# Gated MLP after softcap attention on one core: first queries' transfers on two queues, an early table load, a last fill unit in the scores' banks, another bank for v unit 0

## The chip, the cores and the metric

One NeuronCore of a Trainium2 chip runs the whole kernel. The metric is the device time of one execution in microseconds; a lower number is better. The time before is the median of three runs; a further execution was profiled.

## The reference

Two batches of 12 heads, 448 positions, 64 features per head. Softcap attention, a gMLP block with a spatial gate, and a convolutional gated MLP follow each other:

```python
scores = cap * np.tanh((scale * q @ k.T) / cap)
attn = np.exp(scores - scores.max(-1, keepdims=True))
attn = attn / (attn.sum(-1, keepdims=True) + 1e-09)
x = heads_side_by_side(attn @ v)                       # 448 x 768
h = gelu_tanh(x @ w_in)                                # 448 x 1024
u, v = h[..., :512], h[..., 512:]
v_n = (v - mean(v)) / sqrt(var(v) + 1e-06) * g_ln
x = x + (u * (w_sg @ v_n + b_sg)) @ w_out
h = np.maximum(x @ w2_in, 0.0)
out = h * sigmoid(depthwise_conv3(h, conv_w)) @ w2_out
```

Everything is float32, the weights of the two MLPs float64.

## The kernel before

Every product is made of three TensorE (PE) products: an operand is split into a `hi` part of reduced precision and the `lo` rest, and hi·hi, hi·lo and lo·hi are added up in PSUM. ScalarE (ACT) and VectorE (DVE) make the splits. The float64 weights come in as words in pieces; each piece is decoded by ACT and DVE in three or four operations (`decode`, `decode_half`; tile `f`).

*Attention* works on 12 pairs of heads, two rounds R per pair. `scores` multiplies K by Q into four PSUM banks (tag "sc"), ACT takes the tanh and the exponential (tile `raw`), and `values` multiplies `raw` by V and by ones into three banks (tag "pv"), the sums beside the values. The eighth bank (pool `psm`, tag "mo") is left for other work. The sums are inverted and spread over the partitions by a way through DRAM, but for the last pair, where `norm_pe` inverts them on DVE and `spread` does the spreading by four products on PE; these go to the instruction lists in recording order (`ordered`).

*The head.* `load(0)` starts the transfers of the first pair: Q's two halves (partitions 0 to 63 and 64 to 127) through SP's queue, the first 256 columns of K's halves through ACT's. `WARM` matmuls on a tile of zeros (`wz`) occupy PE until the first operands are ready. `prep_k(0)` splits K on DVE, `prep_q(0)` splits Q with ACT (hi) and DVE (lo), `constants` makes the cap's reciprocal, which scales the first tanh. ACT's first activation brings a table load with it.

*The fill units.* The table FILL puts the first four units of the next product (u = X·w_in, batch 0, i = 0 to 3) between the last rounds of the attention. Unit 1 takes a bank of the scores (`free`, name "fi"), the others the `psm` bank. `u_done` takes the gelu, in four steps, the last on DVE (L231, tile `u`).

*Behind the attention*, `rest` runs a list of units (`seq`): u of batch 0 (the four already done), v units 0 to 2, u of batch 1, v units 3 to 6, eight spatial-gate units (`sg_unit`), twelve output units (`o_unit`). v unit 3, "v3" below, is the one on the gathered last rows of both batches (`XS`, in the tile GH). Each unit takes a bank by `bank(n)`: the one `psm` bank for n < 4 and for n % 4 == 3, the seven of `ps1` else. A v unit is evacuated by ACT (square, L224), DVE (L227), ACT (tanh), DVE (L231), and then normalised; a gate unit by DVE (`gt`), ACT (GH, the hi half) and DVE (`gl`, the lo half), from which the output units multiply. In this part a scheduler that simulates the program's timing sets the order of each engine's instructions, from the recording and the tiles' dependences; `pin` forces an instruction behind another.

In the names of the rows the number of a buffer is left out, and L392 is the one line through which all ordered products go.

Of the kernel before, what the change touches and what calls it, by code (L numbers as in the profile page):

```python
# [37 lines left out]

TAKEN = 4

WARM = 13

K0 = 2 * P

# [9 lines left out]
def stages(  # L54
# [46 lines left out]
    def f(ap):  # L101
        return ap.bitcast(F32)
# [30 lines left out]
    ub = [c0]  # L133

    heads = []

    def decode_half(hi, lo, src, pool, bufs, wait, hi_eng, top_eng):

        n = src.shape[1]
        r = pool.tile([P, 512, 2], U32, tag="f64", name="f64", bufs=bufs)[:, :n]  # L140
        words = r.rearrange("p c w -> p (c w)").bitcast(U16)
        sync(words[:, : 4 * n - 1], src.rearrange("r c w -> r (c w)").bitcast(U16)[:, 1:])
        low = r[:, :, 0]
        top = words.rearrange("p (c w) -> p c w", w=4)[:, :, 2].bitcast(BF16)
        heads.append(heads.pop(0))
        hd = heads[-1][:, :n]

        def s1():
            half = hd.bitcast(F16).rearrange("p (c w) -> p c w", w=2)[:, :, 1]
            with pin(lasta), pin(lastv):  # L150
                if top_eng == "a":
                    A.activation(half, top, AF.Copy)
                else:
                    V.tensor_copy(half, top)

        def s2():
            V.scalar_tensor_tensor(
                out=low, in0=low, scalar=13, in1=hd, op0=ALU.logical_shift_right, op1=ALU.bitwise_or
            )
            if hi_eng == "a":  # L160
                A.activation(hi, f(low), AF.Copy)
            else:
                V.tensor_copy(hi, f(low))

        def s3():
            V.tensor_tensor(out=lo, in0=f(low), in1=f(hi), op=ALU.subtract)

        for k, fn in zip(wait, (s1, s2, s3)):
            later(k, fn)
# [111 lines left out]
    def attention(att, psa):  # L281
# [10 lines left out]
        def load(n):  # L292
            b, p = divmod(n, NPAIR)
            qr = att.tile([P, S], F32, tag="qr", name="qr", bufs=3)
            kr = kraw[n % 2]
            for h in range(2):
                r = slice(h * D, (h + 1) * D)
                sync(qr[r], qT[b, p, r, h])

            k0 = 0 if n else K0  # L300
            if k0:
                nc.scalar.dma_start(kr[:D, :k0], kT[b, p, :D, 0, :k0])
                nc.scalar.dma_start(kr[D:, :k0], kT[b, p, D:, 1, D : D + k0])
            sync(kr[:D, k0:], kT[b, p, :D, 0, k0:])
            sync(kr[D:, k0:ST], kT[b, p, D:, 1, D + k0 :])
            sync(kr[D:, ST:], kT[b, p, D:, 1, :D])
            qraw[n] = qr, kr
# [9 lines left out]
        def prep_q(n):  # L317
            qr, _ = qraw[n]
            q = Qt[n] = att.tile([P, 2, S], F32R, tag="Q", name="Q", bufs=2)
            if n == 0:  # L320

                lasta[0] = A.activation(q[:, 0], qr, AF.Copy)  # L322
                with pin(lastv):
                    lastv[0] = V.tensor_tensor(out=q[:, 1], in0=qr, in1=f(q[:, 0]), op=ALU.subtract)
                return
            V.tensor_scalar(out=q[:, 0], in0=qr, scalar1=qscale[:, 0:1], scalar2=None, op0=ALU.mult)
            lastv[0] = V.scalar_tensor_tensor(
                out=q[:, 1], in0=qr, scalar=qscale[:, 0:1], in1=f(q[:, 0]),
                op0=ALU.mult, op1=ALU.subtract,
            )  # L330
# [28 lines left out]
        if WARM:  # L359

            wz = att.tile([P, S], F32R, tag="rb", name="wz", bufs=2)
            V.memset(f(wz), 0.0)
            wps = psa.tile([P, 4, 512], F32, tag="sc", name="wps", bufs=1)[:, 0, :S]
            for i in range(WARM):
                T.matmul(wps, lhsT=wz[:, :P], rhs=wz, start=True, stop=True)
        prep_k(0, slice(0, K0))
        prep_q(0)
        constants(att)
        creg = A.alloc_register("creg")
        with pin(lasta):  # L370
# [27 lines left out]
        def scores(N, half, then=None):  # L398
# [28 lines left out]
            for g in range(2 * half, 2 * half + 2):  # L427
# [3 lines left out]
                c = slice(g * P, (g + 1) * P)  # L431
                if g < 3:

                    for i, (j, l) in enumerate(((0, 0), (1, 0), (0, 1)) if N == 0 else ((0, 0), (0, 1), (1, 0))):
                        for h in range(2):
                            r = slice(h * D, (h + 1) * D)
                            out, x = to[:, g * 2 + h, :S] if g < 2 else ps[:, h, :2], q[r, l]
# [152 lines left out]
        def norm_pe(N, both):  # L590

            b, p = divmod(N, NPAIR)
            both_e = att.tile([P, 2 * (S + HS)], F32, tag="E", name="E", bufs=3)[:, S + HS :]
            A.activation(both_e, both, AF.Copy)
            e, r = both_e[:, :S], both_e[:, S:]
            V.tensor_scalar(out=r, in0=r, scalar1=guard, scalar2=None, op0=ALU.add)
            V.reciprocal(out=r, in_=r)

            def spread():
                rp = sums[:, :S]  # L600
# [14 lines left out]
        for R in range(2 * NN + LAGS[1] + 1):  # L615
# [40 lines left out]
            if R in FILL:  # L656

                i, k0, k1 = FILL[R]
                if k0 == 0:
                    if i == 1:  # L660
                        free = psa.tile([P, 4, 512], F32, tag="sc", name="fi", bufs=1)
                    fill[i] = free[:, i, :S] if i == 1 else psm.tile([P, 512], F32, tag="mo", name="mo")[:, :S]
                for k in range(k0, k1):
                    mmw(fill[i], 0, i, k, ordered)
                if k1 == NK:
# [81 lines left out]
    def rest():  # L747
# [3 lines left out]
        with ExitStack() as s1:  # L751
# [16 lines left out]
                G.tensor_copy(XS[:, :, :, b * D : (b + 1) * D], f(X[:, :, :, b, ST:S]))  # L768

            def bank(n):  # L770
                return (psm if n < 4 or n % 4 == 3 else ps1).tile([P, 512], F32, tag="mo", name="mo")

            ub.append(c1)

# [312 lines left out]
```

## Time and profile before

| what | value |
|---|---|
| median of 3 runs | 326.25 us (325.84 to 326.45) |
| the profiled execution's own time | 326.67 us |
| its span | 324.9 us |
| PE busy | 315.0 us, 97% |
| DVE busy | 243.5 us, 75% |
| ACT busy | 219.8 us, 68% |
| share of PE in the chain that ended last | 94% |

The span is the time from the first to the last instruction that the profiler recorded; 1.8 us of the execution's own time lie outside it. A busy share is an average over stages: a stage's own limit is read from the rows of that stage, and the chain that ended last shows which wait was the last to end. Start times are counted from the span's start.

### The profile page before, as it was taken

The page shows a single profiled execution, that of the slowest core. Times are in us where ns is not written, and L with a number is a line of the kernel's source. Part 1 is how long each engine was busy: PE and PEld are TensorE (multiplying, and loading weights), DVE is VectorE, ACT ScalarE, POOL GpSimd, SP SyncE. Part 2 cuts the span into 40 slices and gives each one's busy share as a digit, 9 for nine tenths or more (in the row PEclk, how much of TensorE's full clock was granted, in tenths as well). Part 3 has the DMA queues.
Part 4 walks back from the last instruction along what each step waited for, and adds up shares of the span by engine and source line. Part 5 has one row for each costly group of instructions (what it writes and reads, how often), then busy time and mean ns, then how long its engine had stood idle before and what let it go on. Part 6 is the DMA issues. An engine that isn't in the chain of part 4 may idle for free.

```text
span 324.9 us, 6285 instructions
## 1 busy us (share of the span) xinstructions
PE 315.0 (97%) x2377; PEld 260.8 (80%) x2377; DVE 243.5 (75%) x485; ACT 219.8 (68%) x353; POOL 36.5 (11%) x73
## 2 busy tenths in 40 slices
PE   6999999999999999999999999999999999999992
PEld 5566666666677789988999999999999999999991
DVE  2749698598576899999997889996788999990000
ACT  2999999898973457767765655555667988883010
POOL 4001042241341120211111000000000000000000
PEclk9999999999999999999999999999999999999998
DMA  3567976955542253122223670002490123013111
GB/s 111 133 197 207 248 217 145 247 150 179 168 126 69 59 167 108 50 69 95 67 72 126 203 295 0 2 1 65 130 372 19 32 67 97 1 55 141 63 59 34
DMA packets 22222, 37.73 MB, mean 116 GB/s; under 512 B 7352, under 2 KB 14536, under 8 KB 22184
## 3 DMA queue, kind: packets, MB, share of 16 engines
q1 hardware_dynamic: 20392, 34.51, 34.8%
q0 software_dynamic: 1632, 2.61, 2.9%
q8 instruction: 20, 0.33, 0.4%
q14 instruction: 18, 0.15, 0.2%
q10 hardware_dynamic: 160, 0.13, 0.1%
HBM read 34.40 MB, written 2.79 MB: 114 GB/s over the span
## 4 chain that ended last, share of the span: by engine, by line
PE 94%; ACT 2%; DMA 1%; DVE 1%; SPq 0%; issue 0%; ACTq 0%
PE mo L114 18%; PE mo L112 18%; PE mo L113 18%; PE pv L392 15%; PE sc L392 10%; PE mo L392 4%; PE mo L791 3%; PE mo L793 3%; PE mo L792 3%; DMA qr<-in_qT_dram 1%; PE fi L392 1%; ACT raw L409 1%; PE mo L837 1%; PE mo L838 0%; ACT L322 0%; DVE u L231 0%
## 5 line engine op out<-in xcount | busy, mean ns | idle before, releaser
L113 PE MATMUL mo<-X,WI 128*128 128x448 f32 x120 | 43.7, 366 | 0.0
L114 PE MATMUL mo<-X,WI 128*128 128x448 f32 x120 | 43.7, 365 | 0.0
L112 PE MATMUL mo<-X,WI 128*128 128x448 f32 x120 | 43.1, 366 | 0.0
L418 ACT ACTIVATE raw<-raw 128x1344 f32<-128x1344 f32 (+2 forms) x25 | 36.4, 1461 | 0.7
L114 PE MATMUL mo<-HG,W 128*128 128x448 f32 x96 | 34.7, 365 | 0.0
L113 PE MATMUL mo<-HG,W 128*128 128x448 f32 x96 | 34.6, 366 | 0.0
L409 ACT ACTIVATE raw<-sc 128x1792 f32<-128x1792 f32 (+1 forms) x22 | 32.5, 1475 | 2.0 <-PE sc L392 1.8
L112 PE MATMUL mo<-HG,W 128*128 128x448 f32 x96 | 33.3, 366 | 0.0
L392 PE MATMUL pv<-raw,V 128*32 128x224 f32 x576 | 32.9, 358 | 0.0
L182 ACT ACTIVATE f<-f 128x256 f32<-128x256 f32 (+2 forms) x44 | 22.9, 520 | 12.9 <-DMA f<-in_w_in_dram 7.1
L192 DVE SCALAR_TENSOR_TENSOR f<-f 128x256 uint32<-128x256 uint32 (+2 forms) x44 | 22.4, 518 | 9.2 <-ACT f L185 8.9
L392 PE MATMUL sc<-Q,K 64*128 64x448 f32 x210 | 27.7, 385 | 0.4 <-ACT raw L409 0.4
L392 PEld LDWEIGHTS pv<-raw,V 128*32 128x32 f32 x576 | 18.8, 109 | 11.6 <-issue 5.5
L392 PEld LDWEIGHTS sc<-Q,K 64*128 64x128 f32 x210 | 17.9, 185 | 9.7 <-ACT raw L409 5.5
L112 PEld LDWEIGHTS mo<-X,WI 128*128 128x128 f32 x120 | 22.5, 188 | 1.9
L113 PEld LDWEIGHTS mo<-X,WI 128*128 128x128 f32 x120 | 22.5, 188 | 1.9
L114 PEld LDWEIGHTS mo<-X,WI 128*128 128x128 f32 x120 | 22.5, 188 | 1.8
L185 ACT ACTIVATE f<-f 128x256 uint32<-128x256 uint32 (+2 forms) x44 | 22.6, 514 | 0.0
L195 DVE SCALAR_TENSOR_TENSOR f<-f 128x256 uint32<-128x256 uint32 (+2 forms) x44 | 22.4, 514 | 0.1
L971 ACT ACTIVATE o<-mo 128x448 f32<-128x448 f32 x12 | 6.3, 543 | 22.3 <-PE mo L114 18.9
L112 PEld LDWEIGHTS mo<-HG,W 128*128 128x128 f32 x96 | 18.0, 188 | 1.6
L114 PEld LDWEIGHTS mo<-HG,W 128*128 128x128 f32 x96 | 18.0, 188 | 1.4
(155 smaller groups left out, 694.9 us busy)
## 6 DMA issues: line engine op xcount, KB each, us to landing
f<-in_w_in_dram SPq DMA_DIRECT2D x12, 512.0 KB, 4.0
f<-in_w_out_dram SPq DMA_DIRECT2D x24, 256.0 KB, 5.0
f<-in_w_in_dram SPq DMA_DIRECT2D x12, 511.8 KB, 5.8
f<-in_w_out_dram SPq DMA_DIRECT2D x8, 384.0 KB, 3.1
qr<-in_qT_dram SPq DMA_DIRECT2D x24, 112.0 KB, 4.3
out_dram<-o SPq DMA_DIRECT2D x12, 224.0 KB, 2.0
rb<-d POOLq DMA_DIRECT2D x22, 112.0 KB, 3.5
V<-in_vL_dram SPq DMA_DIRECT2D x12, 192.0 KB, 3.4
```

The source lines that it names most:

```text
L112: matmul(ps, lhsT=whi, rhs=xhi, start=start, stop=False)
L113: matmul(ps, lhsT=whi, rhs=xlo, start=False, stop=False)
L114: matmul(ps, lhsT=wlo, rhs=xhi, start=False, stop=stop)
L182: A.activation(f(h), f(h), AF.Copy, scale=2.0**-112)
L185: A.activation(l, l, AF.Copy, scale=0.93 * 2.0**-29)
L192: V.scalar_tensor_tensor(out=l, in0=h, scalar=3, in1=l, op0=ALU.logical_shift_left, op1=ALU.bitwise_or)
L195: V.scalar_tensor_tensor(out=l, in0=h, scalar=0x80000000, in1=l, op0=ALU.bitwise_and, op1=ALU.bitwise_or)
L392: lastm[0] = T.matmul(*args, **kw)
L409: lasta[0] = A.activation(x, ps, AF.Tanh, **sc)
L418: lasta[0] = A.activation(x, x, AF.Exp, scale=creg)
L791: T.matmul(ps, lhsT=xs(0, k), rhs=WI[1][:, 0, k], start=k == 0, stop=False)
L792: T.matmul(ps, lhsT=xs(0, k), rhs=WI[1][:, 1, k], start=False, stop=False)
```

## The change

Eight edits:

1. `load(0)` starts Q's half 0 through ACT's queue and half 1 through SP's, each as the first of its queue; the K halves come second, half 0 through ACT's, half 1 through SP's.
2. A one-column exponential of the zeros is recorded right behind their memset, so that the table load stands there.
3. `prep_q(0)` is recorded ahead of `prep_k(0)`, which is pinned behind Q's lo half on DVE; the first pair's products take hi·hi, K hi·Q lo, K lo·Q hi, as the other pairs do.
4. `WARM` goes from 13 to 12.
5. Fill unit 3 takes bank 3 of `free` in place of the `psm` bank.
6. `bank(n)` gives the `psm` bank to n = 4 too, which is v unit 0.
7. In `norm_pe` the copy of the last pair's sums is pinned behind ACT's last pinned activation.
8. The second step of `decode_half` is pinned behind the last pair's reciprocal, once that is recorded.

```diff
--- before.py
+++ after.py
@@ -38,7 +38,7 @@
 
 TAKEN = 4
 
-WARM = 13
+WARM = 12
 
 K0 = 2 * P
 
@@ -133,6 +133,7 @@
     ub = [c0]
 
     heads = []
+    drain = [None]
 
     def decode_half(hi, lo, src, pool, bufs, wait, hi_eng, top_eng):
 
@@ -154,9 +155,10 @@
                     V.tensor_copy(half, top)
 
         def s2():
-            V.scalar_tensor_tensor(
-                out=low, in0=low, scalar=13, in1=hd, op0=ALU.logical_shift_right, op1=ALU.bitwise_or
-            )
+            with pin(drain):
+                V.scalar_tensor_tensor(
+                    out=low, in0=low, scalar=13, in1=hd, op0=ALU.logical_shift_right, op1=ALU.bitwise_or
+                )
             if hi_eng == "a":
                 A.activation(hi, f(low), AF.Copy)
             else:
@@ -293,14 +295,14 @@
             b, p = divmod(n, NPAIR)
             qr = att.tile([P, S], F32, tag="qr", name="qr", bufs=3)
             kr = kraw[n % 2]
+            k0 = 0 if n else K0
             for h in range(2):
                 r = slice(h * D, (h + 1) * D)
-                sync(qr[r], qT[b, p, r, h])
-
-            k0 = 0 if n else K0
-            if k0:
-                nc.scalar.dma_start(kr[:D, :k0], kT[b, p, :D, 0, :k0])
-                nc.scalar.dma_start(kr[D:, :k0], kT[b, p, D:, 1, D : D + k0])
+                dma = sync if n or h else nc.scalar.dma_start
+                dma(qr[r], qT[b, p, r, h])
+                if k0:
+                    dma(kr[r, :k0], kT[b, p, r, h, D * h : D * h + k0])
+
             sync(kr[:D, k0:], kT[b, p, :D, 0, k0:])
             sync(kr[D:, k0:ST], kT[b, p, D:, 1, D + k0 :])
             sync(kr[D:, ST:], kT[b, p, D:, 1, :D])
@@ -320,8 +322,7 @@
             if n == 0:
 
                 lasta[0] = A.activation(q[:, 0], qr, AF.Copy)
-                with pin(lastv):
-                    lastv[0] = V.tensor_tensor(out=q[:, 1], in0=qr, in1=f(q[:, 0]), op=ALU.subtract)
+                lastv[0] = V.tensor_tensor(out=q[:, 1], in0=qr, in1=f(q[:, 0]), op=ALU.subtract)
                 return
             V.tensor_scalar(out=q[:, 0], in0=qr, scalar1=qscale[:, 0:1], scalar2=None, op0=ALU.mult)
             lastv[0] = V.scalar_tensor_tensor(
@@ -360,11 +361,13 @@
 
             wz = att.tile([P, S], F32R, tag="rb", name="wz", bufs=2)
             V.memset(f(wz), 0.0)
+            A.activation(guard, f(wz[:, :1]), AF.Exp)
             wps = psa.tile([P, 4, 512], F32, tag="sc", name="wps", bufs=1)[:, 0, :S]
             for i in range(WARM):
                 T.matmul(wps, lhsT=wz[:, :P], rhs=wz, start=True, stop=True)
-        prep_k(0, slice(0, K0))
         prep_q(0)
+        with pin(lastv):
+            prep_k(0, slice(0, K0))
         constants(att)
         creg = A.alloc_register("creg")
         with pin(lasta):
@@ -431,7 +434,7 @@
                 c = slice(g * P, (g + 1) * P)
                 if g < 3:
 
-                    for i, (j, l) in enumerate(((0, 0), (1, 0), (0, 1)) if N == 0 else ((0, 0), (0, 1), (1, 0))):
+                    for i, (j, l) in enumerate(((0, 0), (0, 1), (1, 0))):
                         for h in range(2):
                             r = slice(h * D, (h + 1) * D)
                             out, x = to[:, g * 2 + h, :S] if g < 2 else ps[:, h, :2], q[r, l]
@@ -591,10 +594,11 @@
 
             b, p = divmod(N, NPAIR)
             both_e = att.tile([P, 2 * (S + HS)], F32, tag="E", name="E", bufs=3)[:, S + HS :]
-            A.activation(both_e, both, AF.Copy)
+            with pin(lasta):
+                lasta[0] = A.activation(both_e, both, AF.Copy)
             e, r = both_e[:, :S], both_e[:, S:]
             V.tensor_scalar(out=r, in0=r, scalar1=guard, scalar2=None, op0=ALU.add)
-            V.reciprocal(out=r, in_=r)
+            drain[0] = V.reciprocal(out=r, in_=r)
 
             def spread():
                 rp = sums[:, :S]
@@ -659,7 +663,7 @@
                 if k0 == 0:
                     if i == 1:
                         free = psa.tile([P, 4, 512], F32, tag="sc", name="fi", bufs=1)
-                    fill[i] = free[:, i, :S] if i == 1 else psm.tile([P, 512], F32, tag="mo", name="mo")[:, :S]
+                    fill[i] = free[:, i, :S] if i % 2 else psm.tile([P, 512], F32, tag="mo", name="mo")[:, :S]
                 for k in range(k0, k1):
                     mmw(fill[i], 0, i, k, ordered)
                 if k1 == NK:
@@ -768,7 +772,7 @@
                 G.tensor_copy(XS[:, :, :, b * D : (b + 1) * D], f(X[:, :, :, b, ST:S]))
 
             def bank(n):
-                return (psm if n < 4 or n % 4 == 3 else ps1).tile([P, 512], F32, tag="mo", name="mo")
+                return (psm if n < 5 or n % 4 == 3 else ps1).tile([P, 512], F32, tag="mo", name="mo")
 
             ub.append(c1)
```

The edits also move instructions that they don't name, since the scheduler sets the order. Three places follow; line numbers of the changed kernel are up to four higher.

DVE around its first operation on v3, the row of L227 (`gs` is a v unit's tile, `g` a u unit's, `f` and `WO` belong to a piece of w_out), before:

```order
L195 SCALAR_TENSOR_TENSOR f_1705<-f_1705 128x384
L204 TENSOR_TENSOR WO<-f_1703,WO 128x384
L803 BN_STATS bs<-gs 128x6
L231 SCALAR_TENSOR_TENSOR u<-g_1789,mo 128x448
L227 SCALAR_TENSOR_TENSOR gs<-gs,mo 128x512
L204 TENSOR_TENSOR WO<-f_1705,WO 128x384
L804 BN_AGGR mv<-bs 128x2
L805 TENSOR_SCALAR mv<-mv 128x1
L812 SCALAR_TENSOR_TENSOR gs<-gs,mv,gbc 128x512
L231 SCALAR_TENSOR_TENSOR gs<-gs,mo 128x512
L192 SCALAR_TENSOR_TENSOR f_1797<-f_1797 128x384
```

and now (L227 is L229, and the operation on v3 is the first of the two marked x2):

```order
L809 TENSOR_SCALAR mv<-mv 128x1
L816 SCALAR_TENSOR_TENSOR gs<-gs,mv,gbc 128x512
L229 SCALAR_TENSOR_TENSOR g_1788<-g_1788,mo 128x448
L197 SCALAR_TENSOR_TENSOR f_1704<-f_1704 128x384
L233 SCALAR_TENSOR_TENSOR u<-g_1753,mo 128x448
L206 TENSOR_TENSOR WO<-f_1702,WO 128x384
L824 SCALAR_TENSOR_TENSOR VN<-gs,mv,VN 128x512
L233 SCALAR_TENSOR_TENSOR u<-g_1788,mo 128x448
L206 TENSOR_TENSOR WO<-f_1704,WO 128x384
L229 SCALAR_TENSOR_TENSOR gs<-gs,mo 128x512 x2
L233 SCALAR_TENSOR_TENSOR gs<-gs,mo 128x512
L807 BN_STATS bs<-gs 128x6
```

The aggregation, the two operations on `mv` and `gs`, VN's lo half and one of WO's lo halves stood behind v3's first operation and now stand ahead of it. On PE, v3's own eighteen products stand 26 matmuls later in the list than before.

PE where the first output unit begins (products of GH and `gl` with WO; those of WS with VN are gate units'), before:

```order
L114 MATMUL mo<-WS_1521,VN 128x448
L112 MATMUL mo<-GH,WO 128x448
L113 MATMUL mo<-gl,WO 128x448
L114 MATMUL mo<-GH,WO 128x448
L112 MATMUL mo<-GH,WO 128x448
L112 MATMUL mo<-WS_1521,VN 128x448
L113 MATMUL mo<-WS_1522,VN 128x448
L112 MATMUL mo<-WS_1521,VN 128x448
L113 MATMUL mo<-WS_1522,VN 128x448
L112 MATMUL mo<-WS_1521,VN 128x448
L113 MATMUL mo<-WS_1522,VN 128x448
```

and now:

```order
L114 MATMUL mo<-WS_1520,VN 128x448
L112 MATMUL mo<-GH,WO 128x448
L113 MATMUL mo<-gl,WO 128x448
L114 MATMUL mo<-GH,WO 128x448
L112 MATMUL mo<-GH,WO 128x448
L113 MATMUL mo<-gl,WO 128x448
L114 MATMUL mo<-GH,WO 128x448
L112 MATMUL mo<-WS_1520,VN 128x448
L113 MATMUL mo<-WS_1521,VN 128x448
L112 MATMUL mo<-WS_1520,VN 128x448
```

Before, four products of the output unit were followed by eight of the gate units; the second `gl` product now comes right behind the first three.

ACT around the first split of GH (L182 and L185, now L184 and L187, decode a piece of w2_in), before:

```order
L228 ACTIVATE gs<-gs 128x512
L182 ACTIVATE f_1861<-f_1861 128x512
L185 ACTIVATE f_1861<-f_1861 128x512
L819 ACTIVATE VN<-gs,mv 128x512
L108 ACTIVATE GH<-gt 128x448
L182 ACTIVATE f_1863<-f_1863 128x512
L185 ACTIVATE f_1863<-f_1863 128x512
L224 ACTIVATE gs<-mo 128x512
L199 ACTIVATE WI_76<-f_1861 128x512
L108 ACTIVATE GH<-gt 128x448
```

and now:

```order
L230 ACTIVATE gs<-gs 128x512
L184 ACTIVATE f_1860<-f_1860 128x512
L187 ACTIVATE f_1860<-f_1860 128x512
L226 ACTIVATE gs<-mo 128x512
L184 ACTIVATE f_1862<-f_1862 128x512
L187 ACTIVATE f_1862<-f_1862 128x512
L108 ACTIVATE GH<-gt 128x448 x2
L230 ACTIVATE gs<-gs 128x512
L201 ACTIVATE WI_76<-f_1860 128x512
```

The split of GH stood between two pieces' decoding; now two splits stand behind both pieces'.

## Rows read from the trace of the kernel before

**Rows 1.** The page, the chain that ended last, share by engine.

```profile
PE 94%; ACT 2%; DMA 1%; DVE 1%; SPq 0%; issue 0%; ACTq 0%
```

**Rows 2.** The chain of waits in the first 15 us: start us, us, what.

```profile
1.37 4.03 DMA qr<-in_qT_dram
...
5.47 1.28 ACT L322
...
6.76 0.58 ACT Q L322
...
7.37 0.62 DVE Q L324
...
8.57 1.01 ACT raw L409
```

**Rows 3.** Timeline of the head: start us, us, engine line operation [idle before <-releaser].

```profile
0.73 0.56 ACTq L302 DMA_DIRECT2D kr<-in_kT_dram  x1
0.73 1.47 SPq L86 DMA_DIRECT2D qr<-in_qT_dram  x2
...
1.38 4.75 PE L365 MATMUL wps<-wz 128*128 128x448 f32 x13 [1.38 <-DVE wz L362]
...
5.02 0.29 DVE L106 CAST K<-kr 128x256 fp32r<-128x256 f32 x1 [3.69 <-DMA kr<-in_kT_dram]
...
8.29 0.15 DVE L263 TENSOR_SCALAR one<-one 128x1 f32<-128x1 f32 x1
...
8.36 0.77 PE L392 MATMUL sc<-Q,K 64*128 64x448 f32 x6
```

**Rows 4.** Timeline at the last fill unit and the last pair's reciprocal.

```profile
106.00 3.94 PE L392 MATMUL mo<-X,WI 128*128 128x448 f32 x18 [0.40 <-DVE u L231]
...
108.15 1.55 DVE L597 RECIPROCAL E<-E 128x224 f32<-128x224 f32 x1
```

**Rows 5.** Busy time by stretch: stretch, its us, each engine's, PEclk, DMA share, GB/s.

```profile
123.00:138.00 15.00, 15.00 (x75) 13.82 (x74) 14.82 (x31) 10.90 (x22) 2.47 (x3) 1.00 0.30 80
...
154.00:186.00 32.00, 32.00 (x159) 29.48 (x158) 27.81 (x54) 19.88 (x36) 2.74 (x3) 1.00 0.37 110
```

**Rows 6.** The same view, over the first burst of transfers.

```profile
2.03:2.93 0.90, 0.90 (x4) 0.82 (x3) 0.00 (x0) 0.00 (x0) 0.90 (x4) 1.00 0.70 196
```

**Rows 7.** Timelines of PE, ACT and DVE around v3.

```profile
141.65 0.39 PE L793 MATMUL mo<-WI,GH 128*128 128x512 f32 x1
...
142.14 0.60 ACT L224 ACTIVATE gs<-mo 128x512 f32<-128x512 f32 x1 [1.00 <-PE mo L793]
...
143.11 0.67 DVE L227 SCALAR_TENSOR_TENSOR gs<-gs,mo 128x512 f32<-128x512 f32 x1
143.71 0.54 DVE L204 TENSOR_TENSOR WO<-f,WO 128x384 fp32r<-128x384 f32 x1
...
145.11 0.68 DVE L231 SCALAR_TENSOR_TENSOR gs<-gs,mo 128x512 f32<-128x512 f32 x1
```

**Rows 8.** Timeline of DVE, the lo halves gl 0, gl 1 and gl 5.

```profile
160.83 0.59 DVE L109 TENSOR_TENSOR gl<-gt,GH 128x448 fp32r<-128x448 f32 x1
...
165.47 0.61 DVE L109 TENSOR_TENSOR gl<-gt,GH 128x448 fp32r<-128x448 f32 x1
...
182.78 0.62 DVE L109 TENSOR_TENSOR gl<-gt,GH 128x448 fp32r<-128x448 f32 x1
```

**Rows 9.** Timeline of PE, the first products of gl 0, gl 1 and gl 5.

```profile
165.75 0.36 PE L113 MATMUL mo<-gl,WO 128*128 128x448 f32 x1
...
168.80 0.37 PE L113 MATMUL mo<-gl,WO 128*128 128x448 f32 x1
...
184.67 0.36 PE L113 MATMUL mo<-gl,WO 128*128 128x448 f32 x1
```

**Rows 10.** Timeline of ACT, where decoding waits for a transfer.

```profile
160.54 0.68 ACT L182 ACTIVATE f<-f 128x512 f32<-128x512 f32 x1 [0.90 <-DMA f<-in_w_in_dram]
...
168.62 0.70 ACT L182 ACTIVATE f<-f 128x512 f32<-128x512 f32 x1 [2.37 <-DMA f<-in_w_in_dram]
```

## The prediction

> **What bounds the kernel now.** I read the page's chain first: 94% of what ended last is TensorE (PE) [rows 1], so only work taken off PE, or a wait in front of it, can show. The view of PE's waits has four entries, two of them over before 1.4 us and at 10.5; the two that the change touches stand in the rows of the head and of the last fill unit. After 106 us PE waits for nothing. So I read two places closely, the head and that fill unit, and then asked whom a PE that runs earlier would overtake.
>
> In the head the chain of waits runs through Q's transfer (to 5.40), the table load (1.28), Q hi on ScalarE (ACT, 0.58), Q lo on VectorE (DVE, 0.62) and the products to the first tanh at 8.57 [rows 2]. The timeline shows why Q is late: its halves stand one behind the other on SP's queue, while K's are alone on ACT's [rows 3]. At the fill unit, PE starts at 106.00 after 0.40 us of waiting for a `u` that DVE makes [rows 4]. And in the stages that follow, DVE is busy 14.82 of 15.00 us (123 to 138) and 27.81 of 32 (154 to 186), while PE has no gap at all [rows 5]: DVE is the engine that has to follow.
>
> **The change, part by part.**
>
> *Head: -1.95 us.* Before, the first burst runs from 2.03 to 2.93 us at 196 GB/s, 176 KB [rows 6]: the size of one K half and one Q half (64 + 112 KB), the first transfer of each queue. In the change both queues start with a Q half, 224 KB; at that rate this takes 1.14 us, to 3.2, the lower bound. The upper bound is Q as late as before less SP's issue of one half, about 0.64 of the 1.47 for two [rows 3]: 4.76. I take 3.7, nearer to the burst. The table load now follows the memset of the warm data, done by 1.38 when PE starts on it [rows 3]; with the one-column activation behind it, it is over before 3 and leaves the path. Q hi then ends at 4.3 and Q lo at 4.95. K is second on each queue; DVE's cast of it began at 5.02 before [rows 3], and I take 4.9 to 5.0 again (bounds 4.0, in a burst right behind Q's, and 5.7). Its hi takes 0.29 and lo 0.42, so K lo ends at about 5.8. Thirteen warm matmuls held PE to 6.13; twelve hold it to some 5.85, a thirteenth of 4.75 being 0.37 and the last ones quicker. Six unhindered products take 0.77 (those at 8.36): the tanh can start at **6.62** instead of 8.57. The constants that it also needs took 0.45 behind Q lo (7.99 to 8.44); behind K lo they are done at 6.3. With K at 5.7 the gain is 1.5; with all at the lower bounds the warm matmuls set it, 2.1. The products' new order only follows DVE's (Q lo ahead of K lo), and costs nothing itself.
>
> *Fill unit 3: -0.40 us.* In the scores' banks it does not wait for `u`; PE's own wait of 0.40 goes [rows 4]. ACT and DVE evacuate it as before.
>
> *The last pair: 0.* The reciprocal (1.55 [rows 4]) goes ahead of the pieces' work on DVE, and PE's spread behind twelve products of the first v unit, 2.4 us of cover at 0.203 each (165.75 to 168.80 is 15 of them [rows 9]). PE had no wait there, so nothing is gained; the pieces behind the reciprocal get back later what they lose now. Without the cover it would cost at most the 1.55.
>
> *The banks from unit 4 on: new waits, +1.6 us.* v unit 0 now takes the single bank; v unit 3 (the one on the gathered rows, "v3") is due in that bank after it, and PE runs v3 26 matmuls later. At 0.203 that is 5.3 us; PE leads by 2.35, so v3's last matmul ends at 141.65 + 0.39 + 5.3 - 2.35 = 145.0. ACT's square takes 0.7 more (to 142.74 before), so DVE's first operation on v3 can start at 145.7. It started at 143.11, with no idle time before it [rows 7]. DVE is in order. Of the work behind it, five instructions now stand ahead: four that took from 143.71 to 145.11 [rows 7], and one over 512 columns like that of 143.11 (0.6), 2.0 in all. DVE thus leaves this place 145.7 - 143.11 - 2.0 = 0.6 us *later* than before, while PE is 2.35 earlier.
>
> PE next needs DVE for the gated lo halves, `gl`. gl 0 ended at 161.42 [rows 8]; plus 0.6 and two more instructions ahead of it (1.3) it ends at 163.3. PE used it at 165.75 [rows 9]; now at 163.4: no wait. gl 1 ended at 166.08; plus 0.6, less three instructions that now stand behind it (1.9): 164.8. Its first use was at 168.80; the first output unit now runs its first six products in one piece, 12 places or 2.45 us sooner: 168.80 - 2.35 - 2.45 = 164.0, a **wait of 0.8**. In the second batch gl 5 ended at 183.40, and PE used it at 184.67; four places sooner, 2.35 earlier and 0.8 given back, that is 182.3: a shortfall of 1.1 if gl 5 keeps its time. DVE's pace there hangs on ACT's decoding, and ACT's on transfers (0.90 at 160.54, 2.37 at 168.62 [rows 10]), which start as buffers come free. I take 0.8 of the 1.1, since a transfer's time does not follow PE by itself. Sum **+1.6**; bounds 0 (DVE and the transfers follow PE everywhere) and 2.5 (the 1.1 in full, and v3's 0.6 felt once more).
>
> *Sum:* -1.95 - 0.40 + 1.6 = -0.75. The profiled execution took 326.67 (span 324.9), 0.42 above the median of the runs: it would take 325.92, and against the median of 326.25 the forecast is **325.5 us**. A difference under 0.2%, 0.65 us (325.6 to 326.9), could not be told from none.
>
> **A rule against the head.** The burst holds 176 KB of two queues at once [rows 6]: two queues' first transfers moved together. The Trainium skill (DMA: Bandwidth & Descriptors, "Issuing engines are not separate DMA queues") says that transfers started by several engines run on the same 16 DMA engines and interleave, and that spreading them only saves the time to issue them. By it, Q would be in hand at 4.76, and the sum would be that of rival B. The trace agrees with the sharing; whether Q gains more than the issue time, because K no longer shares its burst, no row of before shows.
>
> **The rivals.**
>
> A. *No new waits* (20%). DVE catches up: it has 4.2 us of idle time between 154 and 186 [rows 5], and pieces are drawn ahead where v3 is late. Then the whole 2.35 stays: 323.9. Against it: DVE has no idle time before 143.11 [rows 7], and is in order.
>
> B. *Q gains only the issue time* (20%). Q hi ends at 5.37, Q lo at 6.0, K hi and lo behind it on DVE at 6.7, the constants at 7.2; the tanh starts at 7.25, -1.3. v3 shifts with PE, so the waits stay near 1.5: -1.3 - 0.40 + 1.5 = -0.2, 326.05. If Q came no sooner than 5.40 (the change not doing what it says), only part of the table load would go, with the tanh at 7.9: 326.6. Against B: K's half took its share of the first burst and now comes later.
>
> C. *Decoding stops the gating* (13%), the rival that ends slower. In the new order ACT's split of GH for gl 0 stands behind the two decoding activations of one more `w2_in` piece, which wait for that piece's transfer; before, the split came first and the wait of 0.90 after it [rows 10]. A wait there costs PE nothing up to gl's slack, and microsecond for microsecond from there on; the total is slower than before once all new waits pass 2.35. With one more of the length shown (2.37) on top of my 1.6, that is +1.6: 327.85. For it: ACT is in order too. Against it: the transfers are issued ahead as buffers come free, and the longer one was no wait of PE's.
>
> **How the numbers follow.** Forecast (new waits of 1 to 2.3) 47%, A 20%, B 20%, C 13%. Faster by over 0.65 are A, six tenths of the forecast's case (its middle lies 0.1 beyond the bound) and four tenths of B: 0.20 + 0.28 + 0.08 = 0.56. Slower are three quarters of C and an eighth of B: 0.12. The rest, 0.32, is no change. The range reaches from A (323.9, rounded down to 323.8) over the forecast's own (324.9 to 326.2) and B (to 326.6) to 326.7; outside are most of C and the early edge of A, some 2 in 10.
>
> **What would show it.** Right: the table load off the chain, the tanh at 6.5 to 6.8, fill 3 with no idle time before it; then PE waits of about 0.8 us each in front of products on `gl`, near 164 and 182, released by DVE, and an idle gap of DVE before its first operation on v3, near 145. Wrong: the tanh after 7.2 (B); no wait of PE behind 100 us (A); PE waiting for `GH` or `gl` while ACT waits for a transfer (C).

## The result: 2.85 us slower, and the profile after

| | before | after |
|---|---|---|
| median of the runs, us | 326.24 | 329.09 (328.11 to 330.93) |
| profiled execution, us | 326.67 | 330.93 |
| its span, us | 324.9 | 329.1 |
| first product of the first pair starts | 7.39 | 6.16 |
| first gate unit's first product | 154.12 | 153.04 |
| second MLP's first product | 199.02 | 200.16 |
| its last product of the hidden half | 259.73 | 260.90 |
| span's end | 324.88 | 329.07 |

The ratio is 1.0083 [1.0064, 1.0101]: slower, where the forecast was 325.5 and faster. The profiled execution lies 1.84 above the changed kernel's own median, so the trace says where time goes and the medians say how much. By the table PE is 1.08 ahead at 153, 1.14 behind at 200, still 1.17 behind at 261, and 4.19 behind at the end. Time is lost in two places, and both lie behind 106 us, where PE had waited for nothing.

The page of the changed kernel, busy time and chain; against [rows 1], PE's share of the chain fell from 94 to 75%:

```profile
PE 317.0 (96%) x2376; PEld 260.1 (79%) x2376; DVE 244.0 (74%) x485; ACT 219.8 (67%) x354; POOL 40.3 (12%) x73
...
PE 75%; DMA 7%; ACT 6%; DVE 5%; SPq 2%; issue 2%; POOL 1%; ACTq 0%; DVEq 0%
```

Its view of PE's waits (waiting engine, tile and line, what it waited for; us in total, times, longest us):

```profile
PE mo L112 <- ACT HG L108: 1.7, 1, 1.7
PE wps L367 <- DVE wz L363: 1.4, 1, 1.4
PE mo L112 <- ACT VN L823: 1.1, 1, 1.1
PE pv L395 <- DVE sm L472: 0.6, 1, 0.6
PE mo L113 <- DVE gl L109: 0.4, 1, 0.4
PE sc L395 <- ACT raw L412: 0.4, 1, 0.4
```

The rows on `HG`, `VN`, `sm` and `gl` are new. Only the one on `gl` is of the kind that was forecast, at half its size; `VN`, `HG` and `sm` stood in no term of the sum.

Its timeline of the head, to be read against [rows 3]:

```profile
0.73 0.58 SPq L86 DMA_DIRECT2D qr<-in_qT_dram  x1
0.73 0.58 ACTq L302 DMA_DIRECT2D qr<-in_qT_dram  x1
...
1.38 4.85 PE L367 MATMUL wps<-wz 128*128 128x448 f32 x12 [1.38 <-DVE wz L363]
...
2.16 1.28 ACT L364 ACT_TABLE_LOAD   x1 [2.16 <-issue]
...
3.98 0.58 ACT L324 ACTIVATE Q<-qr 128x448 fp32r<-128x448 f32 x1 [0.33 <-DMA qr<-in_qT_dram]
...
5.46 0.42 DVE L109 TENSOR_TENSOR K<-kr,K 128x256 fp32r<-128x256 f32 x1
...
6.16 0.88 PE L395 MATMUL pv<-Q,K 64*128 64x448 f32 x6
...
7.08 1.01 ACT L412 ACTIVATE raw<-pv,one 128x896 f32<-128x896 f32 x1 [2.52 <-PE pv L395]
```

The table load is off the path, Q is split from 3.98, and K's lo half is done by 5.88. PE only comes at 6.16, held by the warm matmuls. The first tanh starts at 7.08 against 8.57 [rows 2].

Its timelines at four later places, in order of time: PE at `sm`, PE at the last fill unit (for [rows 4]), DVE at v3 (for [rows 7]), and PE where the first output unit begins (for [rows 9]), with the operations on POOL and ACT that lead to `VN`:

```profile
42.72 0.59 PE L395 MATMUL pv<-sm,ones 128*32 128x224 f32 x8 [0.61 <-DVE sm L472]
...
104.86 3.94 PE L395 MATMUL fi<-X,WI 128*128 128x448 f32 x18
...
147.52 1.28 DVE L229 SCALAR_TENSOR_TENSOR gs<-gs,mo 128x512 f32<-128x512 f32 x2 [1.92 <-ACT gs L226]
...
164.96 2.04 POOL L812 TENSOR_TENSOR mv<-mv,one 128x1 f32<-128x1 f32 x1 [7.42 <-ACT WI L201]
...
166.04 0.47 PE L113 MATMUL mo<-gl,WO 128*128 128x448 f32 x1 [0.39 <-DVE gl L109]
...
167.03 0.72 ACT L823 ACTIVATE VN<-gs,mv 128x512 fp32r<-128x512 f32 x1 [2.13 <-POOL mv L812]
...
167.80 0.47 PE L112 MATMUL mo<-WS,VN 128*128 128x448 f32 x1 [1.09 <-ACT VN L823]
```

The fill unit starts with no idle time. v3 reaches DVE 4.4 us later than before and after 1.92 of idle time. What DVE then runs late are `gl` and the statistics of the v units, whose ACT half `VN` is finished at 167.75, just before PE takes it. Between DVE's part and `VN` stands one operation on POOL, a power over 128 values. It took 2.04 us here; before, the same operation began at 162.72 and took 0.90.

The same stretches in the view by stage (stretch, its us, each engine's busy us and instructions, PEclk, DMA share, GB/s), of the kernel before:

```profile
164.00:170.00 6.00, 6.00 (x31) 5.54 (x30) 5.72 (x11) 3.42 (x7) 0.00 (x0) 1.00 0.26 87
230.00:240.00 10.00, 10.00 (x51) 9.28 (x50) 7.08 (x15) 5.94 (x15) 0.00 (x0) 1.00 0.80 268
260.00:275.00 15.00, 15.00 (x76) 13.71 (x75) 14.79 (x35) 12.82 (x34) 0.00 (x0) 1.00 0.29 83
275.00:315.00 40.00, 40.00 (x199) 37.09 (x198) 16.87 (x41) 20.34 (x50) 0.00 (x0) 1.00 0.16 61
```

and of the changed one:

```profile
164.00:170.00 6.00, 4.52 (x20) 3.21 (x20) 6.00 (x12) 3.11 (x6) 2.04 (x1) 1.00 0.08 24
230.00:240.00 10.00, 10.00 (x51) 9.25 (x50) 5.57 (x12) 4.56 (x12) 0.00 (x0) 1.00 0.65 209
260.00:275.00 15.00, 13.35 (x66) 11.92 (x65) 14.85 (x35) 13.62 (x36) 0.00 (x0) 1.00 0.19 54
275.00:315.00 40.00, 40.00 (x195) 36.32 (x195) 19.89 (x48) 22.10 (x54) 0.00 (x0) 1.00 0.22 78
```

These rows hold nearly the whole account. PE runs 11, 10 and 4 products fewer in three of the stretches; at 0.203 each that is 2.2, 2.0 and 0.8 us. Less the lead of 1.08 this is 4.0 of the 4.19. The 4 in the last stretch are no wait: its products stand 0.207 apart there, not 0.203. The remaining stretch, 230 to 240, shows the cause of the second loss: PE is full there, and **DVE does 1.5 us less**. At 260 to 275 DVE is full in both kernels (14.8 of 15), so it cannot make that up before PE needs `HG`.

DVE and ACT near 239 in the changed kernel:

```profile
239.13 0.44 ACT L184 ACTIVATE f<-f 128x256 f32<-128x256 f32 x1 [4.06 <-DMA f<-in_w_out_dram]
...
239.92 0.43 DVE L194 SCALAR_TENSOR_TENSOR f<-f 128x256 uint32<-128x256 uint32 x1 [4.19 <-ACT f L187]
...
272.65 0.90 PE L112 MATMUL mo<-HG,W 128*128 128x448 f32 x3 [1.65 <-ACT HG L108]
```

and before:

```profile
234.32 0.43 ACT L182 ACTIVATE f<-f 128x256 f32<-128x256 f32 x1 [2.98 <-DMA f<-in_w_out_dram]
...
235.11 0.43 DVE L192 SCALAR_TENSOR_TENSOR f<-f 128x256 uint32<-128x256 uint32 x1 [1.82 <-ACT f L185]
```

Both wait for the same piece of w2_out, the second MLP's output weights (the rows leave out the digit), the third that is decoded there; in the changed kernel it comes 4.8 us later. The two orders on SP's queue say why. Before and after, DMA issues in SP's order (a piece's number is one lower in the changed kernel; 2494 and 2493 are the piece decoded third, 2558 and 2557 the fourth):

```
L88 DMA f_2450<-in_w_out_dram 128x512
L88 DMA f_2452<-in_w_out_dram 128x512
L88 DMA f_2698<-in_w_out_dram 128x512
L88 DMA f_2494<-in_w_out_dram 128x512
L88 DMA f_2734<-in_w_out_dram 128x512
L88 DMA f_2558<-in_w_out_dram 128x512
```

```
L88 DMA f_2449<-in_w_out_dram 128x512
L88 DMA f_2451<-in_w_out_dram 128x512
L88 DMA f_2697<-in_w_out_dram 128x512
L88 DMA f_2733<-in_w_out_dram 128x512
L88 DMA f_2735<-in_w_out_dram 128x512
L88 DMA f_2805<-in_w_out_dram 128x512
L88 DMA f_2493<-in_w_out_dram 128x512
L88 DMA f_2807<-in_w_out_dram 128x512
L88 DMA f_2557<-in_w_out_dram 128x512
```

The piece decoded third was issued fourth and is now issued seventh, behind three that are needed much later. No edit names it: the scheduler drew up this queue anew when the edits changed the kernel that it orders.

### The profile page after: what moved, and what is told of

Read it like the earlier page. It is cut to its first block, busy times and chain, and to the rows that moved or that the text cites. A ratio compares the mean times of both kernels' runs of the same rounds, so it can differ in the third digit from the quotient of the medians.

```text
span 329.1 us, 6277 instructions
## 1 busy us (share of the span) xinstructions
PE 317.0 (96%) x2376; PEld 260.1 (79%) x2376; DVE 244.0 (74%) x485; ACT 219.8 (67%) x354; POOL 40.3 (12%) x73
## 4 chain that ended last, share of the span: by engine, by line
PE 75%; DMA 7%; ACT 6%; DVE 5%; SPq 2%; issue 2%; POOL 1%; ACTq 0%; DVEq 0%
PE mo L112 14%; PE mo L113 14%; PE mo L114 14%; PE pv L395 12%; PE sc L395 7%; DMA f<-in_w_in_dram 4%; PE mo L795 3%; PE mo L796 3%; PE mo L797 3%; DMA f<-in_w_out_dram 3%; PE mo L395 2%; PE fi L395 2%; SPq L86 2%; PE wps L367 1%; ACT f L187 1%
## 5 line engine op out<-in xcount | busy, mean ns | idle before, releaser
L184 ACT ACTIVATE f<-f 128x256 f32<-128x256 f32 (+2 forms) x44 | 22.7, 517 | 17.2 <-DMA f<-in_w_in_dram 9.4
L194 DVE SCALAR_TENSOR_TENSOR f<-f 128x256 uint32<-128x256 uint32 (+2 forms) x44 | 23.0, 531 | 9.2 <-ACT f L187 9.0
L197 DVE SCALAR_TENSOR_TENSOR f<-f 128x256 uint32<-128x256 uint32 (+2 forms) x44 | 22.9, 527 | 0.2
L187 ACT ACTIVATE f<-f 128x256 uint32<-128x256 uint32 (+2 forms) x44 | 22.5, 512 | 0.0
```

Of the source, the lines that this page charges most:

```text
L184: A.activation(f(h), f(h), AF.Copy, scale=2.0**-112)
L187: A.activation(l, l, AF.Copy, scale=0.93 * 2.0**-29)
L194: V.scalar_tensor_tensor(out=l, in0=h, scalar=3, in1=l, op0=ALU.logical_shift_left, op1=ALU.bitwise_or)
L197: V.scalar_tensor_tensor(out=l, in0=h, scalar=0x80000000, in1=l, op0=ALU.bitwise_and, op1=ALU.bitwise_or)
```

## The experiments

All times are medians of the runs in us, beside those of the kernel before, run on the same chip, with a ratio and its 95% interval; the ratio is worked out from all those runs, so it is not exactly that of the two medians. Diffs are against the changed kernel unless they say otherwise; "old head" and the like mean that the named edits are taken back. Three theories came up on the way: the late place of v3 (V), the number of buffers for the second MLP's pieces (W), and the order on SP's queue (Q).

**Which edits cost: head alone, tail alone, all but the banks, all but fill and banks.**

e1_head_only, edits 1 to 4 (edits 5 to 8 taken back, of which the lines that count are):

```diff
-fill[i] = free[:, i, :S] if i % 2 else ...
+fill[i] = free[:, i, :S] if i == 1 else ...
-return (psm if n < 5 or n % 4 == 3 else ps1)...
+return (psm if n < 4 or n % 4 == 3 else ps1)...
```

> Edits 1 to 4 alone (Q's halves first on two queues, early table load, Q ahead of K, 12 warm matmuls); from 106 us on DVE and ACT keep the order of before. Theory O (the new order behind 106 us makes the waits): the head's 1.49 us stay, less the 0.6 that PE loses near 41 us: 324.8 to 325.5, and no PE wait behind 106 us. Rival L (a PE that leads runs into DVE and the transfers whatever the order): the lead is eaten behind 106 us, 326.0 to 327, with PE waits before gl or HG products.

325.94 against 326.44, 0.9982 [0.9966, 0.9998]. Its tanh started at 6.75, yet only 0.5 is left at the end.

e2_tail_only, edits 5 to 8:

```diff
-WARM = 12
+WARM = 13
...
-A.activation(guard, f(wz[:, :1]), AF.Exp)
```

> Edits 5 to 8 alone (fill unit 3 in the scores' banks, bank(n) with n < 5, the two pins of the last pair); the head as before, behind 106 us DVE and ACT in the order of the changed kernel. Theory O: all the waits of the changed kernel without the head's gain: 329.5 to 330.6. Rival L: less lead, fewer waits: 326 to 328.

330.54 against 326.44, 1.0136 [1.0105, 1.0167]. The waits on `VN` (1.1), `HG` (1.0) and `gl` (0.4) are all there with the old head: the loss does not come from PE being early.

e3_no_bank, all but edit 6:

```diff
-return (psm if n < 5 or n % 4 == 3 else ps1)...
+return (psm if n < 4 or n % 4 == 3 else ps1)...
```

> The changed kernel with bank(n) as before (n < 4). If bank(n) is what makes the bad order: 324.4 to 325.5, with no wait near 165 and 271. If the fill unit's place alone makes one as bad: 327 or more. Rival L: 326 to 327.5.

326.64 against 326.44, 1.0014 [0.9999, 1.0029]. Its view of PE's waits:

```profile
...
PE mo L795 <- DVE u L233: 1.3, 1, 1.3
PE pv L395 <- DMA V<-in_vL_dram: 0.4, 1, 0.4
...
```

The late waits are gone, and one of 1.3 stands at v unit 0: the wait for `u` that edit 5 takes from the fill unit only moves to the next user of the same banks. Edit 6 meets that; the prediction did not say so.

e4_head_pins, edits 1 to 4, 7 and 8:

```diff
-fill[i] = free[:, i, :S] if i % 2 else ...
+fill[i] = free[:, i, :S] if i == 1 else ...
-return (psm if n < 5 or n % 4 == 3 else ps1)...
+return (psm if n < 4 or n % 4 == 3 else ps1)...
```

> Edits 1 to 4 with the two pins of the last pair (7, 8), without 5 and 6; behind 106 us the order is nearly that of before. Theory O: as with edits 1 to 4 alone, within 0.4: 324.8 to 325.6. If the reciprocal ahead of the pieces starves DVE's later work: slower than that by up to 1.55.

325.95, 0.9971 [0.9953, 0.9990], level with e1: the pins cost and bring nothing.

**The two halves of the tail.** Diffs against the kernel before. e5_bank_only:

```diff
-return (psm if n < 4 or n % 4 == 3 else ps1)...
+return (psm if n < 5 or n % 4 == 3 else ps1)...
```

> Edit 6 alone (bank(n) with n < 5); the order of DVE and ACT behind 140 us is nearly that of the changed kernel. Theory O (this edit's order makes the waits): 329.5 to 331, with PE waits near 166 and 271. If it takes the fill unit's move as well to make them: 326 to 327.

331.09 against 326.43, 1.0161 [1.0124, 1.0199]: this one line makes the whole loss (+4.66). Waits on `gl` 1.3 in two pieces and `HG` 1.2.

e6_fill_only:

```diff
-fill[i] = free[:, i, :S] if i == 1 else ...
+fill[i] = free[:, i, :S] if i % 2 else ...
```

> Edit 5 alone (fill unit 3 in the scores' banks). v unit 0 takes a bank of the later pool, which lies over it, and waits for its evacuation: minus 0.4 plus the 1.3 that PE waited for u at 111 us in the run without edit 6: 327.0 to 327.6. If the order that it brings costs nothing and the wait is covered: 325.8 to 326.2.

327.06, 1.0016 [1.0000, 1.0033]: alone it gains nothing, its 0.4 returns as a wait of v unit 0 on `u` at 111.88.

**Which unit in the single bank.** Edit 6 makes five units (0, 3, 7, 11 and 15) take turns in one bank.

e7_no_unit7 and e9_no_unit11 (v3 is unit 11):

```diff
-return (psm if n < 5 or n % 4 == 3 else ps1)...
+return (psm if n < 5 or n % 4 == 3 and n > 7 else ps1)...    # e7
+return (psm if n < 5 or n % 4 == 3 and n != 11 else ps1)...  # e9
```

> The changed kernel, but unit 7 (u 0 of batch 1) in the later pool: the single bank goes from v unit 0 to v unit 3 directly. Theory O, with the chain v 0, u 0, v 3 in one bank as the cause of v 3's late place: v 3 comes earlier on PE, the waits near 165 and 271 go, 324.8 to 325.6. If any use of that bank by v unit 0 does it: 328 to 330.

> The changed kernel, but unit 11 (v 3) in the later pool: the order of DVE and ACT behind 106 us is nearly that of the changed kernel, but v 3 keeps its place on PE (as before, 26 matmuls earlier than in the changed kernel). Theory V (v 3's late place makes DVE stand still and carry the lag on): the idle gap of DVE near 146 and PE's waits near 166 and 271 go, 324.8 to 325.8. Rival D (the order of DVE itself makes the waits): 327.5 to 330.

e7: 325.22 against 326.43, 0.9964 [0.9952, 0.9976], no wait behind 60 us. e9: 328.03 against 326.27, 1.0051 [1.0032, 1.0071]. In e9 v3 is back in its old place on PE and DVE does not idle at it, and still PE waits 0.6 for `VN` and 1.3 for `HG`: **theory V fell** as the main cause. v3's place is worth about 1.1 of the loss by the medians (329.09 to 328.03), but the two ratios' intervals overlap, so this is a rough figure.

e8_mod4, and the same kernel once more as e14_mod4_again:

```diff
-return (psm if n < 5 or n % 4 == 3 else ps1)...
+return (psm if n < 5 or n % 4 == 0 else ps1)...
```

> The changed kernel with the single bank for units 4, 8, 12, ... (every fourth from v unit 0 on) in place of 4, 7, 11, ...: the distance in that bank is never under four. Theory O as before: 324.8 to 325.6, if this order suits DVE; v 3 (unit 11) is then in the later pool. If DVE and the transfers can't follow a leading PE in any order: 326 to 327.5.

> The run with units 4, 8, 12, ... again, on the same chip as the one with the old head: 324.8 to 325.4; if the whole head survives, 1.5 below that run, if the stages behind eat it, 0.3 to 0.8 below.

325.00 against 326.43, 0.9954 [0.9941, 0.9967], and 325.29 against 326.30, 0.9963 [0.9945, 0.9981]. e8 has the **lowest median of all versions** (e7 and e12 come within 0.3, and so does e14). Behind 2 us its view of PE's waits holds one row:

```profile
PE sc L395 <- ACT raw L412: 0.4, 1, 0.4
```

**The head, on top of e8.** The diffs here are against e8. e10_mod4_warm11, e11_mod4_old_transfers (edit 1 taken back), e12_mod4_no_pins (edits 7 and 8 taken back), e13_mod4_old_head (edits 1 to 4 taken back):

```diff
-WARM = 12
+WARM = 11          # e10
...
-dma(qr[r], qT[b, p, r, h])
+sync(qr[r], qT[b, p, r, h])          # e11, and K as before
...
-with pin(drain):          # e12
...
-A.activation(guard, f(wz[:, :1]), AF.Exp)          # e13, and WARM = 13
```

> As the run with the single bank for units 4, 8, 12, ..., with 11 warm matmuls. If the warm matmuls held PE at 6.16, with K lo ready at 5.88: the first tanh 0.25 earlier, at 6.8, and 324.7 to 325.0. If PE then starts before the clock rises and its products are slower: no gain, 324.9 to 325.4.

> As the run with units 4, 8, 12, ..., with the transfers in the order of before (both Q halves on SP's queue, K on ACT's). Q in hand at 5.4 again, K behind it on DVE: first tanh at 7.9 instead of 7.1, total 0.4 to 0.9 slower than that run: 325.4 to 325.9. If the head's lead is lost in the stages behind it anyway: within 0.2 of it.

> As the run with units 4, 8, 12, ..., without the two pins of the last pair (edits 7 and 8). My forecast priced them at nothing: within 0.3 of that run, 324.7 to 325.3. If they bring the last pair's sums in time for PE: slower by up to 1.55.

> Edits 5, 7, 8 and the single bank for units 4, 8, 12, ..., with the head as before. The fill unit's 0.4 and nothing else: 325.7 to 326.1, with no PE wait behind 106 us. If the order itself gains or loses: outside that by more than 0.4.

325.44 (0.9962 [0.9943, 0.9981]), 325.58 (0.9981 [0.9967, 0.9996]), 325.20 (0.9965 [0.9947, 0.9982]) and 325.83 (0.9988 [0.9973, 1.0004]). The whole head is worth 0.54 in medians (e13 to e14). In e11, where the table is loaded early but the transfers are the old ones, Q reached ACT only at 5.34:

```profile
5.34 0.58 ACT L324 ACTIVATE Q<-qr 128x448 fp32r<-128x448 f32 x1 [1.88 <-DMA qr<-in_qT_dram]
```

A warm matmul less (e10) and the pins (e12) change nothing that the intervals tell.

**Buffers or order.** e15_after_8_buffers and e16_after_4_buffers:

```diff
-                    ), 12
+                    ), 8     # e15; 4 in e16
```

> The changed kernel with 8 buffers in place of 12 for the w_out pieces of the last part: the order of DVE and ACT is the same, only fewer transfers are issued at once near 232. Theory W (the burst makes the first pieces land late, and DVE's 4 us near 239 become PE's wait near 271): the idle gap near 239 and the wait shrink, 327.3 to 328.4. Rival (the lag comes from the stages before): 328.6 to 329.6, with the wait near 271 as it is.

> The same with 4 buffers (the order in the second MLP differs in places). Theory W: the first pieces land sooner still, the gap near 239 is under 2 us: 327 to 328.2. Rival: 328.6 or more, and new waits for pieces that are issued too late.

328.91 (1.0072 [1.0044, 1.0099]) and 328.98 (1.0068 [1.0043, 1.0093]). DVE's gap near 240, 4.19 in the changed kernel, is still 4.00 and 3.85, and the piece decoded third is still issued seventh: fewer buffers leave the queue's order and the time as they are, and **theory W fell**. The wait on `HG` is smaller there, 0.2 and 0.1, but not because anything was won: PE had come to the second MLP later than in the changed kernel (at 201.57 and 200.83, not 200.16), so that the same lateness of DVE met it with less idle time.

e17_issue_order lets two pieces go ahead in SP's order, third and fourth, and leaves the rest:

```diff
+            lasts[:] = [None]
...
+                    held = lasts[:]
+                    if len(pieces) in (19, 20):
+                        lasts.clear()
```

> The changed kernel with the w_out pieces of the second MLP issued on SP's queue in the order in which they are decoded (third and fourth in place of seventh and ninth); the first MLP's order of every engine is the same. Theory Q (the place in SP's queue makes the gap): DVE's idle time near 239 goes from 4.19 to 1 to 2 us, PE's wait near 271 goes or is under 0.3, total 327.0 to 328.0. Rival (the lag comes from the first MLP alone): gap shorter but PE's wait near 271 as long as DVE stays behind: 328.6 to 329.4.

327.82 against 326.49, 1.0038 [1.0011, 1.0065], 1.27 below the changed kernel's median. **Theory Q held**: the gap near 239 is gone, DVE is busy 9.33 us between 230 and 240, and `HG` is no longer waited for:

```profile
...
PE mo L112 <- ACT VN L823: 1.1, 1, 1.1
PE pv L395 <- DMA V<-in_vL_dram: 0.5, 1, 0.5
PE mo L113 <- DVE gl L109: 0.4, 1, 0.4
...
```

The size, 1.27, is rougher than the trace: the intervals of the two ratios just touch ([1.0011, 1.0065] here, [1.0064, 1.0101] for the changed kernel). The traces of the other kernels side with theory Q on the gap. Where the piece decoded third is issued third, DVE's gap is 0.84 to 1.37 (e8, e10 to e14); fourth, 1.11 to 2.22 (before, e1, e4); sixth, 2.99 to 3.71 (e3, e6, e7, e9); seventh, 3.85 to 4.63 (the changed kernel, e2, e5, e15, e16). What a gap costs PE is another matter: those of 2.99 to 3.28 in e3, e6 and e7 go with waits on `HG` of 0 to 0.2, the 3.71 in e9 with 1.3.

e18_issue_order_no_unit11 joins e17 and e9:

```diff
-return (psm if n < 5 or n % 4 == 3 else ps1)...
+return (psm if n < 5 or n % 4 == 3 and n != 11 else ps1)...   # and e17's lines
```

> The same, with unit 11 (v 3) in the later pool as in the run that kept v 3's old place (328.03). Theory Q: 326.0 to 327.0, PE's wait near 165 (0.6) is left and the one near 271 gone. Rival: 327.5 to 328.5.

330.01 against 326.49, 1.0085 [1.0055, 1.0115]: slower than was expected. The wait on `HG` stayed away as expected, but in the profiled execution PE waited 2.5 for `GH`. ACT's timeline there:

```profile
188.57 0.65 ACT L184 ACTIVATE f<-f 128x512 f32<-128x512 f32 x1 [3.89 <-DMA f<-in_w_in_dram]
...
189.67 1.03 ACT L108 ACTIVATE GH<-gt 128x448 fp32r<-128x448 f32 x2
```

This is rival C's mechanism at work: the split of GH stands behind the decoding of a piece whose transfer is late. That transfer took 7.7 us from its issue at 180.83, as the first of seven; in e9, with the same order on SP in this MLP, it took 4.3 (180.15 to 184.43), and ACT waited 1.01. Why it took 7.7 stays open. The runs of e18 spread from 326.8 to 331.68, so the execution shown may not stand for all of them.

## Why the prediction was wrong, point by point

**The head, -1.95.** Right in its parts, too large by a quarter: the tanh came 1.49 earlier. Q was split from 3.98 where 3.7 was taken for its transfer, and K was ready as forecast; the step that failed is the warm matmuls, "twelve hold it to some 5.85". The twelve took 4.85, more than the thirteen before, since the quicker ones at the end (0.21 apart from 5.55 on in the trace of before) did not come before the twelfth; they came before the end in e1, where PE was free at 5.83. By the trace's clock records PE's clock rises to its 2.4 GHz level at 5.42 us before, at 6.21 in the changed kernel, and anywhere from 4.37 (e17) to 7.47 (e8) in the thirteen kernels with this whole head, whose first tanh then starts at 6.30 (e17) to 7.67 (e8). The forecast 6.62 lies within that range: the size of this term went with when the clock rose in the execution (4.37 and 6.30 in e17, 5.40 and 6.75 in e1, 6.21 and 7.08 in the changed kernel, 7.47 and 7.67 in e8), which the prediction took as fixed.

A step was missing as well: that the lead lasts. In the changed kernel 0.6 of it is gone by 43 us. DVE's cast of a w_in piece stood at 39.24 after 3.53 us of idle time for its transfer (39.03 after 3.06 before); `sm` stands behind it on DVE and began at the same 41.6 in both, so PE, being earlier, waited. What an earlier PE gains is lost where DVE follows a transfer that is not earlier.

**Rival B, and the rule against the head.** ACT took up Q at 3.98, not at 4.76. Against e11's 5.34, the kernels with e11's other edits took it up at 4.27 (e8) and 4.04 (e14), so 1.07 and 1.30 us earlier, both more than the 0.64 of issue; all thirteen kernels with the whole head did so between 3.74 and 4.27. By what the Trainium skill (DMA: Bandwidth & Descriptors, "Issuing engines are not separate DMA queues") says of spreading issues, only that issue time would have been saved; the trace does not agree here. It does agree with the sharing, and that may be why Q gained more: K's bytes no longer stood in Q's burst. No run separates the two.

**Fill unit 3, -0.40.** Right (104.86, no idle time). But the sum priced edits 5 and 6 as if they were apart: without edit 6 the same wait returns at v unit 0, 0.4 in e6 and 1.3 in e3.

**The last pair, 0.** Right, by e4 against e1 and e12 against e8.

**The banks, +1.6 with bounds 0 and 2.5.** This is the term that failed, in both batches, and e5 shows that it alone is +4.7. In the first, the mechanism was the one described: v3 late, DVE idle in front of it. Its size was not. v3's last product ended at 146.9, not 145.0: 1.3 of that because PE's lead was 1.08 and not 2.35, and 0.6 because the 26 products have 512 columns and stand 0.227 apart, not 0.203. The wait that counted was not `gl` (0.39 for the 0.8) but `VN` (1.09); with the slow first products behind each wait (0.31 instead of 0.20 apart) it is 2.2 in all. `VN` is late twice over: POOL's operation starts 2.2 us later than before, since DVE's part of the statistics in front of it is late, and it takes 2.04 us, not 0.90. Without that second part `VN` would have been ready at 166.6, and PE, which was free at 166.7, would not have waited. e16 agrees, with the same order and no wait on `VN`:

```profile
165.38 0.90 POOL L812 TENSOR_TENSOR mv<-mv,one 128x1 f32<-128x1 f32 x1 [7.70 <-ACT WI L201]
```

There PE runs 24 products from 164 to 170, not 20. The operation took 2.03 or 2.04 in e2, e15 and e17 as well, each with a wait of 1.1 on `VN`, 0.90 in e5, which has none, and 1.50 in e9 and e18, with waits of 0.6 and 0.8. Why its time differs by execution stays open.

The six products in one piece, which the prediction took for the reason, are not enough for the wait on `gl`: e9 begins the first output unit in the same way, with v3 in its old place, and shows none there. Nor do e3 and e7, but they run four gate products behind the first of the six and settle nothing.

In the second batch there was no wait on `gl` 5 at all. The loss sits in the second MLP, for which the sum had no entry. The failed step can be quoted, from what was set against rival C: "the transfers are issued ahead as buffers come free". They are issued in the order that the scheduler wrote, and it had moved the piece decoded third from fourth to seventh. DVE's 4.19 us of idle time at 239.9 cost PE nothing there; they came out 33 us later as the 1.65 on `HG`, because DVE is full from 260 on. Putting two issues ahead in that queue gives 1.27 back (e17).

**The rivals.** A (no new waits) fell. C had the right sign, and its mechanism shows in e18, but not in the changed kernel: no `GH` wait there. The case that came true, a queue's order in a later stage, was not among them.

**What stays open.** Of the +4.1 of the tail (e2), the order on SP accounts for about 1.3 and v3's place for about 1.1; each was measured with the other present, and e18, which was to take both, met a wait of its own. The rest was not separated. That the order of the first MLP's transfers has a part in it is argued only, and POOL's longer operation was not tried by itself. Open too is why PE's products behind the wait on `HG` start 0.207 apart in the changed kernel, in e6 and in e16, and 0.203 apart in e2, e5, e9 and e15, all of which wait there; in the profiled execution of the changed kernel that is some 0.9 us.

## What to carry to other kernels

Where a scheduler writes the order, one changed bank can redraw queues hundreds of microseconds away; compare every queue's order by piece, DMA issues included, not only the engines near the edit. A wait of an in-order engine that is full later on does not show where it happens: look for where that engine next has no slack. And an edit that takes away a wait for a shared resource must be priced with the next user of that resource.

## What the runs showed of the hardware

Behind closely spaced waits PE can lose more than the waits themselves, as its granted clock falls to 0.50, the level of 1.2 GHz. In e15's profiled execution, by stage:

```profile
167.60:168.10 0.50, 0.46 (x1) 0.46 (x2) 0.50 (x2) 0.50 (x2) 0.00 (x0) 0.50 0.00 0
168.10:170.80 2.70, 2.70 (x9) 2.35 (x9) 2.70 (x6) 1.11 (x3) 0.00 (x0) 0.50 0.48 167
```

and in its timeline of PE:

```profile
167.64 0.74 PE L112 MATMUL mo<-WS,VN 128*128 128x448 f32 x1 [1.09 <-ACT VN L823]
168.18 0.57 PE L113 MATMUL mo<-WS,VN 128*128 128x448 f32 x1
168.56 0.57 PE L112 MATMUL mo<-WS,VN 128*128 128x448 f32 x1
```

Products stand 0.37 apart instead of 0.20, for about eight of them: 1.4 us on top of a wait of 1.09. The changed kernel had the same wait, and its clock stayed at 1.00. In e5 the clock fell as well (0.66 from 168 to 171), and in e18 (0.50 from 190.8 to 193.4, behind the wait of 2.5). The runs of e5, e15 and e18 spread more than those of e8 and e14 (4.4 to 4.9 us, not 0.8 to 1.8), and the clock goes with part of that: e18's four runs with a mean granted clock of 0.990 or 0.991 took 330.0 to 331.7 us, its five at 0.994 to 0.997 took 326.8 to 330.05. It is not all of it, since e15 took 331.45 at 0.996 and 330.29 at 0.998.
